# A recurrent attention fused with a squared-ReLU layer: DMA due times in the planner, and the state keys of four chunks by a DMA transpose

## The chip, the cores and the metric

The kernel runs on one core of one Trainium2 chip. The metric is the device time of one execution in microseconds, given as the median of several runs. A core has a matrix engine (PE, with its weight loads shown apart as PEld), a vector engine (DVE), a scalar engine (ACT), GpSimd (POOL), the queue engine SP that issues most DMAs of this kernel, and 16 DMA engines that move the bytes. Each engine takes its instructions in the order of the program; between engines there are semaphores.

## The reference

Four sequences, eight heads, 768 steps, 48 features a head. A gated linear recurrence, then a two-layer MLP on the 3072 tokens with 384 features:

```python
for t in range(S):
    state = alpha[:, :, t, :, None] * state + np.einsum('bhd,bhe->bhde', k[:, :, t], v[:, :, t])
    y[:, :, t] = np.einsum('bhd,bhde->bhe', q[:, :, t], state)
...
x = attn_out.transpose(0, 2, 1, 3).reshape(B * S, H * D)
h = x @ w_in                 # 384 -> 2048
r = np.maximum(h, 0.0)
return (r * r) @ w_out       # 2048 -> 384
```

## The kernel before

**Chunks.** The 3072 tokens are 24 chunks of 128, six to a sequence (chunk s is part c = s mod 6 of its sequence; chunks 5, 11, 17 and 23 are the last of theirs). Inside a chunk the recurrence becomes matrix products. With L the logarithm of alpha and A the exponential of its running sum along the tokens, the scores are (q·A)(k/A)ᵀ under a triangular mask, the state takes (k/A)ᵀv and is then multiplied by A of the last token, and the output is scores·v plus (q·A)·state.

**What a chunk issues, chunk 11 and later (the code calls these raw).** Four loads on SP (`at`, `qt`, `kt`, `vt`, line 371). ACT takes the logarithm of alpha (L396). POOL casts q, k and v to bf16 (L413, L405). Two DMA transposes on SP turn q and k (L416, tile `rawt`). PE forms the running sums twice: `p0` (L435, keys by tokens, one matmul of 384 columns with the triangle as weights, only used for the state) and `pT` (L447, transposed, four matmuls). ACT makes A (L451), 1/A transposed (L454) and, from `p0`, 1/A by tokens (`Ainv`, L466). DVE forms q·A transposed (L507), k/A transposed (L510), and k/A by tokens, `kI` (L505). PE then does the scores (`p2`, tile `sc`), the state update (`ps`, tile `st`, whose weights are `kI`), the product with the previous state (`p3a`, weights from `qkT`, data `sb`) and the masked scores times v (`p3b`). DVE scales the state (L581), ACT copies it to bf16 (L586, `sb`), and ACT copies the output to `xn` (L386). The last chunk of a sequence has no state update, hence no `p0`, `Ainv` and `kI`. Finally `xn` is turned into columns of `xT_big`: by PE and DVE for most chunks, by a DMA transpose on SP (L620) for chunks 18 to 22.

**The MLP.** Tokens go in groups: one of four chunks, two of one, then pairs (8 and 9, and so on to 22 and 23). The first product (weights `w_in_b`, tile `bank<-xT_big,w_in_b`) needs the `xT_big` columns of every chunk of the group. ACT applies ReLU (L676), DVE squares into `gT` (L684), and the second product (`bank<-w_out_b,gT`) is copied out (L758) and stored.

**What sets the order.** A small planner in the kernel sorts every operation before anything is emitted. An operation has an engine, a duration, a latency, the operations it waits for and, where it uses PSUM, a bank. The planner starts on each engine what can start first and gives it a finish time, `op.done = t + op.dur + op.lat`. Loads are a first-in first-out engine "DMA", transposes an engine "TR" whose duration also occupies "DMA"; on the chip both go to SP's one queue. After the planning the operations are sorted by start and emitted, so an engine's order on the chip is the planner's. An operation's `late` is added to its place in the sort alone, not to its finish:

```python
op.start = t + getattr(op, "late", 0.0)
free[eng] = t + op.dur
...
op.done = t + op.dur + op.lat
```

So a longer latency in the planner moves what waits for a DMA further back in the order of its engine; the DMA itself is not slower. A gate holds `p0` (or `pT`, where there is no `p0`) of chunk s back until s is at most LEAD plus the number of MLP tiles done, counting a first and a second product as half a tile each:

```python
return s <= LEAD + (prog["m1"] + prog["m2"]) / 5.12
```

Of the kernel before, what the change touches and what calls it, by code (L numbers as in the profile page):

```python
# [54 lines left out]
def after(op, x=0.0):  # L55
    return (op, x)
# [85 lines left out]
def kernel(  # L142
# [10 lines left out]
    nc = tc.nc  # L153
# [4 lines left out]
    NP = H // 2  # L158
# [35 lines left out]
        out=utri_f, in_=utri_f, compare_op=ALU.is_ge, fill=0.0,  # L194
# [10 lines left out]
    for c in range(JN):  # L205
        blk = slice(JP * c, JP * c + JP)
        nc.gpsimd.affine_select(
            out=tri4[blk, 0:JW], in_=tri4[blk, 0:JW], compare_op=ALU.is_ge, fill=0.0,
# [27 lines left out]
    def pin(ins):  # L236
        tc.keep_in_program_order(ins)
# [12 lines left out]
    GLA_BANKS = sl_bank[0:2]  # L250
# [7 lines left out]
    X_SLACK = 0.2  # L258
    LD = 0.98
    LD1 = 1.0  # L260
    WLD = 2.1
    LAG = 3.2
    SQ_PRIO = 0.0

    def add(eng, dur, emit, *deps, **kw):
        return plan.add(Op(eng, dur, emit, deps, **kw))
# [6 lines left out]
    def load_w(which):  # L273
# [25 lines left out]
        prev = w_cast[-SB] if len(w_cast) >= SB else None  # L299
        ld = add("DMA", WLD * n / 4 + 0.03, e_issue, prev, lat=LAG if which == "o" else 2.0)  # L300
        op = add({"POOL": 0.1 + 0.46 * n, "DVE": 0.1 + 0.2 * n, "ACT": 0.1 + 0.32 * n}, 0, e_cast, ld, prio=-3.0)
# [9 lines left out]
    EARLY = 4  # L311
    RAW = 11
    XTURN = (18, 23)
    TLD, TLAT, TLATE = 1.0, 4.0, 2.0
    NR = 3
    R = {}

    def raw_tiles():
        if R:
            return  # L320
        R["b"] = stage.tile([P, NR, 2, H, DP], BF16, name="rawb", tag="stage")
        nc.gpsimd.memset(R["b"][:, :, :, :, D:], 0.0)
        R["t"] = stage.tile([P, NR, 2, NP, P], BF16, name="rawt", tag="stage")
        R["i"] = stage.tile([P, 2, NP, P], BF16, name="aiT", tag="stage")

# [38 lines left out]
    def add_load(s, nm):  # L364
        d = C[s]
        b, c = divmod(s, NCH)

        def ld():
            if nm not in d:
                d[nm] = loads.tile([P, H, D], FP32, name=nm)  # L370
            pin(nc.sync.dma_start(out=d[nm], in_=SRC[nm][b, c]))
        prev = C[s - LB].get("use_" + nm) if s >= LB else None
        d["ld_" + nm] = add("DMA", LD if s < 4 else LD1, ld, prev, lat=2.0 if s < 4 else LAG if s < 6 else 2.4, at=0.6)

    def add_chunk(s):
        d = C[s]
        b, c = divmod(s, NCH)
        i = s % NBUF
        L, qA, kI, ae = L_s[:, i], qA_s[:, i], kI_s[:, i], ae_s[:, i]
        old = C[s - NBUF].get("end") if s >= NBUF else None  # L380
        g = dict(prio=-10.0 + s * 0.01)
        last = c == NCH - 1

        def cast(op, out_t, in_t):
            if op.eng == "ACT":
                pin(nc.scalar.copy(out_t, in_t))  # L386
            elif op.eng == "DVE":
                pin(nc.vector.tensor_copy(out_t, in_t))  # L388
            else:
                pin(nc.gpsimd.tensor_copy(out_t, in_t))  # L390
# [6 lines left out]
        if joint:  # L397
            ln = J["ln"]
        else:
            ln = [add("ACT", 0.41, e_ln, d["ld_at"], old, prio=-15.0 if s < EARLY else -5.0)]  # L400
# [6 lines left out]
        raw = s >= RAW  # L407
        if raw:
            w, wz = s % NR, s % 2

            def e_rb(j, nm):
                raw_tiles()
                pin(nc.gpsimd.tensor_copy(R["b"][:, w, j, :, 0:D], d[nm]))  # L413

            def e_turn(j):
                pin(nc.sync.dma_start_transpose(out=R["t"][:, w, j], in_=R["b"][:, w, j].rearrange("p h d -> p (h d)")))  # L416
            rt = []
            for j, nm in enumerate(["qt", "kt"]):
                cb = add("POOL", 0.55, lambda j=j, nm=nm: e_rb(j, nm), d["ld_" + nm],
                         *([C[s - NR]["turn"][j]] if s >= RAW + NR else []), prio=-5.0)  # L420
                d["use_" + nm] = cb
                t_ = add("TR", TLD, lambda j=j: e_turn(j), cb, *([C[s - NR]["turned"][j]] if s >= RAW + NR else []), lat=TLAT)
                t_.late = TLATE
# [17 lines left out]
        p0 = Op("PE", 0.66 if joint else 0.17 if raw else 0.27, e_p0, ln, takes=GLA_BANKS, lat=0.05, **g)  # L441
# [14 lines left out]
        def e_aeT(j):  # L456
            rows = slice(64 * j, 64 * j + 64)
            pin(nc.scalar.activation(ae[rows, :, j], d["pmT"][rows, :, P - 1], AF.Exp))
# [11 lines left out]

        def e_ae1():
            pin(nc.scalar.activation(ae[64:128, :, 1], d["pm"][64:128, HD:HD + NP], AF.Exp))
        if not (raw and last):
            plan.add(p0)
        if not raw:
            a_ = add("ACT", 0.38, e_A, p0, **g)
            ai = add("ACT", 0.38, e_Ai, p0, after(a_), **g)
        if raw:
            ai = None
            if not last:  # L480
                ai = add("ACT", 0.38, e_Ai, p0, **g)
                p0.gives = ai
            pT = Op("PE", 0.23, e_pT, [*ln] + ([] if last else [after(p0)]), takes=GLA_BANKS, **g)
            plan.add(pT)
            if last:
                pT.gla = s
            aT = add("ACT", 0.48, e_AT, pT, after(ai) if ai else None, **g)
            aiT = add("ACT", 0.48, e_AiT, pT, after(aT), *([C[s - 2]["turned"][1]] if s >= RAW + 2 else []), **g)
            pT.gives = aiT
            if not last:  # L490
                ae0 = add("ACT", 0.18, lambda: e_aeT(0), pT, after(aiT), **g)
                pT.gives = ae1 = add("ACT", 0.19, lambda: e_aeT(1), pT, after(ae0), **g)
        elif joint:
            ae1 = J["ae"]
            p0.gives = ai
        else:
            ae0 = add("ACT", 0.18, e_ae0, p0, after(ai), **g)
            ae1 = add("ACT", 0.19, e_ae1, p0, after(ae0), **g)
            p0.gives = ae1
# [8 lines left out]

        def e_kiT():
            pin(nc.vector.tensor_mul(d["qkT"][:, NP:2 * NP, :], R["t"][:, w, 1], R["i"][:, wz]))  # L510
        if raw:
            if not last:
                mk = d["use_kt"] = add("DVE", 0.47, e_kI, ai, d["ld_kt"], old, **g)
            cp = add("DVE", 0.34, e_qAT, aT, rt[0], **g)
            cpk = add("DVE", 0.34, e_kiT, aiT, rt[1], cp, **g)
            d["turned"] = [cp, cpk]
        else:
            mq = d["use_qt"] = add("DVE", 0.47, e_qA, a_, d["ld_qt"], old, **g)
            mk = d["use_kt"] = add("DVE", 0.47, e_kI, ai, d["ld_kt"], old, **g)
# [11 lines left out]
        if not raw:  # L531
            p1q = plan.add(Op("PE", 0.22, e_p1q, [mq], takes=GLA_BANKS, **g))
            p1k = plan.add(Op("PE", 0.22, e_p1k, [mk] if s < EARLY else [mk, after(p1q)], lat=0.15,
                              takes=P1K_BANKS if s < EARLY else None, **g))

        def e_cp(lo, hi):
            if "qkT" not in d:
                d["qkT"] = work.tile([P, 2 * NP, P], BF16, name="qkT")
            cast(cpk if lo else cp, d["qkT"][:, lo:hi, :], d["pTk"][:, 0:NP, :] if lo else d["pT"][:, lo:hi, :])
        if s < EARLY:  # L540
            cp = add({"ACT": 0.49, "DVE": 0.34}, 0, lambda: e_cp(0, NP), p1q, **g)
            cpk = add({"DVE": 0.34, "ACT": 0.49}, 0, lambda: e_cp(NP, 2 * NP), p1k, **g)
# [23 lines left out]
        if not last:  # L566
# [7 lines left out]
            prev = C[s - 1].get("sb") if s else None  # L574
            if c == 0 and s:
                prev = C[s - 2]["sb"]
# [41 lines left out]
        if XTURN[0] <= s < XTURN[1]:  # L618
            def e_xt():
                pin(nc.sync.dma_start_transpose(out=xT_big[:, :, s * P:(s + 1) * P], in_=d["xn"]))  # L620
            d["x"] = add("TR", 0.8, e_xt, xn, lat=TLAT)
            d["x"].late = 1.0
            d["end"] = xn
            return
        p4 = plan.add(Op("PE", 0.165, e_p4, [xn], takes=GLA_BANKS, lat=0.14, **g))
# [159 lines left out]
    for d in DMA_ORDER + list(range(6, NT)):  # L785
        if d in ("i", "o"):
            load_w(d)
        elif d == "at":
            add_joint_alpha()
        elif isinstance(d, tuple):  # L790
            add_load(*d)
            if d[0] >= JN:
                if all("ld_" + nm in C[d[0]] for nm, _ in srcs):
                    add_chunk(d[0])
            elif d == JLAST:
                for s in range(JN):
                    add_chunk(s)
        else:
            for nm, _ in srcs:
                if nm != "at":  # L800
                    add_load(d, nm)
                elif d <= 9:
                    add_load(d, nm)
                if nm == "at" and 9 <= d < NT - 1:
                    add_load(d + 1, nm)
            add_chunk(d)
# [24 lines left out]
                b2 = add_last(g, tt, b2, pools) if GT[g] + tt == NT - 1 else add_moe2(g, tt, b2, {}, range(NQ), pools)  # L831
        sq[(g, "free")] = b2

    LEAD = 3.7

    def gate(op):
        s = getattr(op, "gla", None)
        if s is not None:
            return s <= LEAD + (prog["m1"] + prog["m2"]) / 5.12
        return True  # L840
# [18 lines left out]
    for op in plan.order:  # L859
        if op.eng == "PE":  # L860
# [3 lines left out]
            if pe_end is not None and DUMMY and not opened and op.start < CALM:  # L864
                n = max(0, int((op.start - pe_end) / 0.11 + (0.4 if op.start < DENSE else -1.8))) + (extra.pop(0) if extra else 0)
# [35 lines left out]
```

## Time and profile before

| What | Value |
|---|---|
| Median of 3 runs | 186.39 us (184.87 to 186.94) |
| The profiled execution's own time | 185.07 us |
| Its span, first to last instruction | 183.4 us |
| PE busy | 177.5 us (97%), 1908 matmuls |
| DVE, ACT, POOL busy | 127.1, 126.5, 39.4 us |
| SP's hardware queue, share of the 16 DMA engines | 80.7% over the span |
| DMA transposes on SP | 26 of `rawt` (median 3.4 us to landing), 5 of `xT_big` (2.5 us) |

The span leaves out 1.7 us of the device time. The records of matmuls overlap, because each shows its whole way through the array; a 384-column matmul has a record of 326 ns, but the next one starts 0.16 us later. So a busy PE is read by the distances between starts, not by the lengths. Rows of SP are times in which SP issues a DMA, not the time that the data takes; the landing is a separate number.

### The profile page before, as it was taken

What the parts mean: (1) busy time and instruction counts of PE and PEld (TensorE: products, weight loads), DVE (VectorE), ACT (ScalarE), POOL (GpSimd) and SP (SyncE); (2) the same over time, 40 slices, a digit from 0 to 9 for tenths busy, and PEclk for the clock granted to TensorE, in tenths of its full rate; (3) what the DMA queues carried; (4) which work ended last, traced back from release to release, by engine and by line L of the source; (5) the groups of instructions that cost most, each with busy time, mean ns of one, the idle gap of its engine ahead of it and who ended that gap; (6) DMA issues with size and microseconds to landing.
All of it is one profiled execution on the core that took longest, in us unless ns stands there. A gap on an engine that the chain in (4) does not pass through costs nothing.

```text
span 183.4 us, 4946 instructions
## 1 busy us (share of the span) xinstructions
PE 177.5 (97%) x1908; PEld 130.5 (71%) x1908; DVE 127.1 (69%) x273; ACT 126.5 (69%) x286; POOL 39.4 (21%) x80
## 2 busy tenths in 40 slices
PE   7999999899999999999999998999999999999993
PEld 2577884567769877867768776667766777778663
DVE  1179898684999998778877867748855984744200
ACT  3677799226859996966967859847975895767321
POOL 8221100021131142132223133342323512000000
PEclk9999999999999999999999999999999999999999
DMA  5999999999999999998999599898898898901022
GB/s 168 215 212 252 302 366 321 326 220 204 177 191 201 194 179 173 141 190 161 150 193 202 113 240 186 161 227 162 170 201 182 176 163 194 301 13 43 12 77 86
DMA packets 120200, 34.12 MB, mean 186 GB/s; under 512 B 112400, under 2 KB 118928, under 8 KB 120176
## 3 DMA queue, kind: packets, MB, share of 16 engines
q1 hardware_dynamic: 119536, 31.83, 80.7%
q0 software_dynamic: 640, 1.97, 3.2%
q8 instruction: 15, 0.25, 0.6%
q14 instruction: 9, 0.07, 0.2%
HBM read 25.17 MB, written 4.72 MB: 163 GB/s over the span
## 4 chain that ended last, share of the span: by engine, by line
PE 49%; DMA 2%; ACT 1%; issue 0%; DVE 0%
PE bank L240 45%; DMA at<-in_alpha_dram 2%; PE sc L240 2%; PE st L240 1%; PE bank L243 1%; ACT aiT L454 0%; ACT r L676 0%; ACT ob L758 0%; ACT L_s L396 0%; ACT ob L716 0%; DVE xT_big L388 0%; ACT qkT L451 0%
## 5 line engine op out<-in xcount | busy, mean ns | idle before, releaser
L240 PE MATMUL bank<-xT_big,w_in_b 128*128 128x256 bf16 (+2 forms) x636 | 76.6, 262 | 0.9 <-ACT r L676 0.7
L240 PE MATMUL bank<-w_out_b,gT 128*128 128x384 bf16 (+1 forms) x400 | 71.6, 320 | 0.5 <-DVE w_out_b L296 0.5
L676 ACT ACTIVATE r<-bank 128x512 bf16<-128x512 f32 x96 | 56.6, 606 | 11.3 <-PE bank L240 9.9
L240 PEld LDWEIGHTS <-w_in_b 128*128 128x128 bf16 x636 | 52.7, 98 | 10.6 <-issue 1.5
L240 PEld LDWEIGHTS <-gT 128*128 128x128 bf16 x416 | 37.2, 98 | 18.7 <-DVE w_out_b L296 1.0
L684 DVE TENSOR_TENSOR gT<-r 128x512 bf16<-128x512 bf16 x96 | 41.8, 453 | 10.2 <-ACT r L676 9.0
L561 DVE TENSOR_TENSOR sm<-sc,utri_b 128x512 bf16<-128x512 f32 x48 | 30.8, 684 | 5.9 <-PE sc L240 5.7
L405 POOL CAST vb<-vt 128x384 bf16<-128x384 f32 x24 | 13.6, 569 | 69.1 <-DMA vt<-in_v_dram 55.2
L386 ACT CAST xn<-bank 128x384 bf16<-128x384 f32 x24 | 11.6, 482 | 11.6 <-PE bank L240 11.5
L505 DVE TENSOR_TENSOR kI_s<-kt,Ainv 128x384 bf16<-128x384 f32 x21 | 12.8, 611 | 7.8 <-ACT Ainv L466 7.8
L240 PEld LDWEIGHTS <-qkT 64*128 64x128 bf16 (+1 forms) x272 | 10.7, 95 | 6.4 <-issue 2.4
L586 ACT CAST sb<-st 128x384 bf16<-128x384 f32 x20 | 9.6, 482 | 7.7 <-DVE st L581 7.5
L758 ACT COPY ob<-bank 128x384 f32<-128x384 f32 x14 | 6.7, 480 | 8.0 <-PE bank L240 8.0
L396 ACT ACTIVATE L_s<-at 128x384 bf16<-128x384 f32 x20 | 10.5, 527 | 2.4 <-DMA at<-in_alpha_dram 2.3
L240 PE MATMUL bank<-warm 128*128 128x256 bf16 (+1 forms) x54 | 10.9, 348 | 1.3 <-DVE warm L188 1.3
L502 DVE TENSOR_TENSOR qA_s<-qt,A 128x384 bf16<-128x384 f32 x11 | 6.3, 575 | 8.0 <-ACT A L462 8.0
L413 POOL CAST rawb<-qt 128x384 bf16<-128x384 f32 x13 | 7.4, 570 | 20.3 <-DMA qt<-in_q_dram 20.3
L413 POOL CAST rawb<-kt 128x384 bf16<-128x384 f32 x13 | 7.6, 587 | 19.0 <-DMA kt<-in_k_dram 11.1
L581 DVE TENSOR_TENSOR st<-st,ae_s 128x384 f32<-128x384 f32 x20 | 11.1, 556 | 0.5 <-PE st L240 0.5
L466 ACT ACTIVATE Ainv<-bank 128x384 bf16<-128x384 f32 x21 | 10.5, 501 | 1.1 <-PE bank L240 1.0
L240 PE MATMUL sc<-qkT 64*128 64x128 bf16 x192 | 9.5, 219 | 0.0
L240 PEld LDWEIGHTS <-sm 128*128 128x128 bf16 x192 | 8.1, 96 | 1.7 <-issue 0.2
(64 smaller groups left out, 165.7 us busy)
## 6 DMA issues: line engine op xcount, KB each, us to landing
qt<-in_q_dram SPq DMA_DIRECT2D x24, 192.0 KB, 4.0
kt<-in_k_dram SPq DMA_DIRECT2D x24, 192.0 KB, 3.6
vt<-in_v_dram SPq DMA_DIRECT2D x24, 192.0 KB, 3.8
at<-in_alpha_dram SPq DMA_DIRECT2D x20, 192.0 KB, 4.0
wo<-in_moe_w_out_dram SPq DMA_DIRECT2D x4, 768.0 KB, 8.5
out_dram<-ob POOLq DMA_DIRECT2D x10, 192.0 KB, 3.1
wi<-in_moe_w_in_dram SPq DMA_DIRECT2D x4, 384.0 KB, 5.3
wi<-in_moe_w_in_dram SPq DMA_DIRECT2D x2, 768.0 KB, 8.3
```

The costliest lines, as they stand in the source:

```text
L240: pin(nc.tensor.matmul(*a, **kw))
L386: pin(nc.scalar.copy(out_t, in_t))
L396: pin(nc.scalar.activation(L[:, :, 0:D], d["at"], AF.Ln))
L405: pin(nc.gpsimd.tensor_copy(d["vb"], d["vt"]))
L413: pin(nc.gpsimd.tensor_copy(R["b"][:, w, j, :, 0:D], d[nm]))
L466: pin(nc.scalar.activation(d["Ai"], d["pm"][:, 0:HD].rearrange("p (h d) -> p h d", h=H), AF.Exp, scale=-1.0))
L505: pin(nc.vector.tensor_mul(kI[:, :, 0:D], d["kt"], d["Ai"]))
L561: pin(nc.vector.tensor_mul(d["sm"][:, hh], d["sc"][:, hh], utri_b.to_broadcast([P, NP, P])))
L581: pin(nc.vector.tensor_mul(st4, st4, bcast(ae, D)))
L586: pin(nc.scalar.copy(d["sbt"], d["st"]))
L676: pin(nc.scalar.activation(box["r"][:, 0:w], box["ph"][:, 0:w], AF.Relu))
L684: pin(nc.vector.tensor_mul(gT[g][:, f0:f0 + per, lo * P:lo * P + n], r, r))
```

## The change

The planner's numbers first. Loads of chunk 11 and later get a latency of 4.2 instead of 2.4 (alpha 5.2), transposes 6.0 instead of 4.0. The transposes of `xn` take a place in SP's order 2.6 after their due start instead of 1.0. LEAD goes from 3.7 to 4.3.

Then chunks 18 to 21. They no longer have `p0`, `Ainv` and the DVE product `kI` (L505). The gate moves to their `pT`. Instead, once DVE has written k/A transposed into `qkT` (L510), SP issues a DMA transpose of it into the same `kI` buffer, with all 64 columns a head, and `ps` waits for that DMA. In the planner it costs 0.65 and lands 6.0 later.

```diff
+    LT = 4.2
...
-    TLD, TLAT, TLATE = 1.0, 4.0, 2.0
+    TLD, TLAT, TLATE, XLATE = 1.0, 6.0, 2.0, 2.6
+    KTURN = 17
...
-        d["ld_" + nm] = add("DMA", LD if s < 4 else LD1, ld, prev, lat=2.0 if s < 4 else LAG if s < 6 else 2.4, at=0.6)
+        d["ld_" + nm] = add("DMA", LD if s < 4 else LD1, ld, prev, lat=2.0 if s < 4 else LAG if s < 6 else 2.4 if s < RAW else LT + (1.0 if nm == "at" else 0.0), at=0.6)
...
+        kd = KTURN <= s < 22 and not last
+        nat = not (s >= RAW and (last or kd))
...
-        if not (raw and last):
+        if nat:
             plan.add(p0)
...
-            if not last:
+            if nat:
                 ai = add("ACT", 0.38, e_Ai, p0, **g)
-            pT = Op("PE", 0.23, e_pT, [*ln] + ([] if last else [after(p0)]), takes=GLA_BANKS, **g)
+            pT = Op("PE", 0.23, e_pT, [*ln] + ([after(p0)] if nat else []), takes=GLA_BANKS, **g)
             plan.add(pT)
-            if last:
+            if not nat:
                 pT.gla = s
...
+        def e_kn():
+            pin(nc.sync.dma_start_transpose(out=kI.rearrange("p (n a) d -> p n (a d)", a=2),
+                                            in_=d["qkT"][:, NP:2 * NP, :].rearrange("p n t -> p (n t)")))
         if raw:
-            if not last:
+            if nat:
                 mk = d["use_kt"] = add("DVE", 0.47, e_kI, ai, d["ld_kt"], old, **g)
...
+            if kd:
+                mk = add("TR", 0.65, e_kn, cpk, old, lat=TLAT)
+                mk.late = 0.5
...
             d["x"] = add("TR", 0.8, e_xt, xn, lat=TLAT)
-            d["x"].late = 1.0
+            d["x"].late = XLATE
...
-    LEAD = 3.7
+    LEAD = 4.3
```

## The prediction

> **What bounds the kernel now.** I read the page's busy line and slices first, to see which engine is full and where.
>
> ```profile
> span 183.4 us, 4946 instructions
> PE 177.5 (97%) x1908; PEld 130.5 (71%) x1908; DVE 127.1 (69%) x273; ACT 126.5 (69%) x286; POOL 39.4 (21%) x80
> PE   7999999899999999999999998999999999999993
> DMA  5999999999999999998999599898898898901022
> ```
>
> PE is full from the second slice to the last, so time can only be won by work taken off PE or by waits of PE; DMA is nearly as full until slice 35 (about 160 us). The waits of PE alone, from the list of waits, show how little is left:
>
> ```profile
> PE bank L240 <- DVE warm L188: 1.3, 1, 1.3
> PE bank L240 <- ACT r L676: 0.7, 1, 0.7
> PE bank L240 <- DVE w_out_b L296: 0.5, 1, 0.5
> PE bank L243 <- DVE kI_s L505: 0.2, 1, 0.2
> ```
>
> The first and third belong to the start (warm-up, and 32 us), which the change leaves alone. The second is the one place where the chain leaves PE in the stretch that it touches; the chain in order of time, 104 to 112 us, says why:
>
> ```profile
> 105.28 4.13 DMA at<-in_alpha_dram
> 109.40 0.02 issue
> 109.42 0.34 ACT L_s L396
> ...
> 110.70 0.60 ACT aiT L454
> 111.30 0.49 ACT r L676
> 111.79 0.04 issue
> 111.84 0.38 PE bank L240 x2
> ```
>
> Chunk 19's alpha was issued at 105.28, landed at 109.40, and ACT, whose order puts its logarithm there, stood still; the ReLU behind it came late for PE. The second full resource is SP. Its timeline, with start and length of each issue:
>
> ```profile
> 128.73 1.47 SPq L416 DMA_TRANSPOSE rawt<-rawb  x1
> 130.25 0.57 SPq L371 DMA_DIRECT2D kt<-in_k_dram  x1
> 130.92 1.21 SPq L620 DMA_TRANSPOSE xT_big<-xn  x1
> 132.18 0.57 SPq L371 DMA_DIRECT2D vt<-in_v_dram  x1
> 132.80 0.58 SPq L371 DMA_DIRECT2D at<-in_alpha_dram  x1
> 133.49 1.84 SPq L416 DMA_TRANSPOSE rawt<-rawb  x1
> 135.37 0.58 SPq L371 DMA_DIRECT2D qt<-in_q_dram  x1
> 136.06 1.90 SPq L416 DMA_TRANSPOSE rawt<-rawb  x1
> 138.06 1.23 SPq L620 DMA_TRANSPOSE xT_big<-xn  x1
> ```
>
> Each row begins within 0.1 us of the last one's end, and so it goes from 63 to 155 us; the only gaps are 1.36 us at 149 and 0.96 us at 154. An issue of a load takes 0.57 us, of a transpose 1.2 to 3.5 (mean 1.70 over the 26 of `rawt`).
>
> **The change part by part.** *Removed from PE:* `p0` of four chunks. For chunk 18, PE's timeline has it at 121.84 and the next matmul at 122.00, so 0.16 us; 4 × 0.16 = **0.65 us**, all on the path, since PE is full around it. *Removed from ACT and DVE:* four `Ainv` and four `kI`,
>
> ```profile
> L505 DVE TENSOR_TENSOR kI_s<-kt,Ainv 128x384 bf16<-128x384 f32 x21 | 12.8, 611 | 7.8 <-ACT Ainv L466 7.8
> L466 ACT ACTIVATE Ainv<-bank 128x384 bf16<-128x384 f32 x21 | 10.5, 501 | 1.1 <-PE bank L240 1.0
> ```
>
> 4 × 0.50 = 2.0 us of ACT and 4 × 0.61 = 2.4 us of DVE. From 120 to 150 us both are busy for 21 to 22 of 30 us, so I count this at nothing: it is idle time made longer. Without that cover it would be worth up to 2 us.
>
> *Later due times for loads.* Alpha gets 2.8 us more before its logarithm is placed, q, k and v 1.8 more before POOL's casts. Against the 0.71 us that ACT stood idle at 109.4 that is enough, so the wait of 0.66 us at 111.8 should go: **−0.66 us** (bounds 0, if another late landing takes its place, and −0.66). What is late next is the casts and with them the transposes of q and k, which can take it: from the landings of the `rawt` rows and the starts of L510, keys of chunks 18 to 23 landed at 118.5, 124.5, 131.9, 139.6, 146.0, 153.8 and were first used at 124.5, 131.0, 138.4, 144.3, 151.0, 157.2, so 3.4 to 6.5 us early.
>
> *LEAD.* By counting product matmuls in the timeline, `p0` of chunk 19 ran at 128.2 when 16.9 first and 13.75 second tiles were done, a lead of 19 − 15.3 = 3.7; chunks 9 to 22 all show 3.6 to 3.7. The gate binds, and 0.6 tile more, at some 6.6 us a tile (`xn` of 18 to 22 are 6.6 apart), would let a chunk start 4.0 us earlier. But in the planner the turned keys come 1.8 + 2.0 = 3.8 us later, which uses up nearly the same 4 us. So I expect chunks to run 0 to 2 us earlier up to about 20 and up to 2 us later at 22 and 23. That costs no PE time while there is second-product work to put in: when the first product of tiles 18, 20 and 22 began (141.0, 154.3, 163.3), second products were 1.5, 1.5 and 2.5 tiles behind, at 16 × 0.162 = 2.6 us each, a cover of 3.9, 3.9 and 6.5 us. **0.**
>
> *Four key transposes.* Shape and type are those of a `rawt` transpose. DMA engines: the queue moved 31.83 MB in 80.7% of 183.4 us, 215 GB/s, so 128 KB take 0.61 us; four make 2.4 us, where the share from 120 to 150 us is 0.87, which leaves 3.9. SP: each takes 1.2 to 3.5 us of a queue without gaps; with the mean and the 0.08 between rows, 4 × 1.78 = 7.1 us, less the two gaps of 2.3, puts its tail up to 4.8 us later; at the minimum of 1.2, 4 × 1.28 − 2.3 = 2.8. Behind them queue the turned q and k of chunks 20 to 23, the last loads, and the `xn` transposes. The Trainium skill, "Advanced Engine Details and Errata", section "X-Bar Transpose (TRN2)", states that transpose DMAs are as fast as regular ones. By that rule I would estimate 4 × 0.65 = 2.6 us on SP, hidden but for 0.3; the issue rows here do not agree with it (1.70 against 0.57), though the landings do (3.4 us against 3.6 to 4.0).
>
> *The new wait.* `ps` of chunks 18 to 21 now waits for a DMA that begins after L510, and behind it on PE wait the whole MLP and the next chunks. Before, `ps` came about 1 us after L510 (124.5, 125.5). The state is next needed by `p3a` of the following chunk, at 133.4 for chunk 19, so the planner may put `ps` up to 6 us back without harm; it budgets 6.65 us. The nearest rows land 2.3 to 5.9 us after issue (median 3.4), plus the wait in SP's queue, which for `rawt` I read as about 2 us from cast end to issue: typically 5.4, at worst 8. So 0 for three chunks and about one miss of 0.3: **+0.3 us** (bounds 0 and 4 × 1.3 = 5.2).
>
> *The transposes of `xn`.* The `x` of chunk 19 landed at 140.5 and its first product began at 141.0; of 21 at 154.2 and 154.3. These are exactly in time, so lateness here is paid by PE. The change gives 2.0 us more time and places the issue 1.6 us later, so 0.4 net, plus the 0 to 2 us of earlier chunks; against it stands SP's push of 2.8 to 4.8 us by the end. I take **+0.2 us** (bounds 0 and +4.4, the whole push less 0.4), near the low end because the landing rows (2.5 us) are far under the 6.0 now allowed.
>
> **Sum:** −0.65 − 0.66 + 0.3 + 0.2 = −0.8 us. On the profiled execution 185.07 becomes 184.3 (span 182.6). The shown median is 1.32 us above the profiled run; carrying the same difference over, 186.39 − 0.8 = **185.6 us**.
>
> **Rivals.** *Slower: SP's queue decides.* If every key transpose costs SP its mean of 1.78 us and SP can't catch up, two of them lie ahead of chunk 19's `x` or the next (3.6 us) and all four ahead of chunk 21's; PE, in order, stands at the first product of tiles 18 and 20. Less 0.4 of net allowance, that is about 3.2 us at the first and, because PE is then itself later, 1.2 more at the second: 186.39 − 1.3 + 4.4 = 189.5 in full, 188.6 with 0.9 us earlier chunks. It decides from about 3.2 us of waits on. For it: SP has no gaps, and `x` lands in the last moment today. Against: many of SP's long rows contain waits for casts that later due times shorten.
>
> *Faster by more.* The three runs differ by 2.1 us for one program, and the profiled one is near the lowest. If the 1.3 us between it and the median are waits for late landings like the one at 105 us, and the new due times hold them off: 186.39 − 0.65 − 0.66 − 1.3 = 183.8. For it: a load landing between 2.9 and 8.8 us. Against: PE shows almost no such waits, and nothing shown says where the other runs lose.
>
> *It does not bring the lead that it says.* The gate's 4 us and the keys' 3.8 us cancel, another load is late in place of alpha's, and the 0.65 us are spent in waits for keys: 186.4, no change.
>
> **How the numbers follow.** Forecast 0.37, no change 0.10, faster by more 0.25, slower 0.28. A measurement of this kernel can tell about 1% (1.9 us) from nothing. Forecast and no change fall within it (0.47), the other two outside. The range reaches from 183.4, just under the faster case, to 188.9, past the middle of the slower one; the forecast's own range is 184.6 to 186.6.
>
> **What would show it.** Right: no `Ainv` or `p0` at chunks 18 to 21; PE waits near 111 us gone; keys landing within 6 us of L510; `ps` without a wait; SP without gaps and ending near 158 to 160 us rather than 157. Wrong: a PE wait released by a DMA at `st<-vb,kI_s` or at the first product of tiles 18, 20 or 22 totalling over 2 us, key transposes that take SP over 2 us each, or PE waits in new places with the old ones kept.

## The result and the profile after

The change makes the kernel slower. Its median is 187.3 us (185.99 to 188.46, six runs) against 185.2 us for the kernel before in the same set (183.76 to 186.94); the ratio is **1.0137, interval 1.0095 to 1.018**. In this and all comparisons below a ratio leaves out executions more than 1.5% above the fastest of their kernel, so a median can stand further off than its ratio says. The profiled execution took 186.69 us, span 185.0.

The page after, busy line and two rows of the slices:

```profile
span 185.0 us, 4923 instructions
PE 176.0 (95%) x1904; PEld 129.7 (70%) x1904; DVE 124.2 (67%) x270; ACT 124.8 (67%) x281; POOL 38.8 (21%) x80
PE   7799998899999999999999999999998999999993
DMA  5999999999998999979999998798889998941012
```

The work went as foretold: four matmuls fewer, and four `kI` on DVE and four `Ainv` on ACT (the page has three and five records fewer, because one copy of an output moved from ACT to DVE). The span is 1.6 us longer, and PE is busy 1.5 us less. Both numbers have to be split before they are read. Up to the scores of chunk 8 both kernels give PE the same work in the same order, and this execution is already 0.7 us behind there (60.35 instead of 59.69 us); the first 7 us alone have 1.0 us less of busy PE. From that point on the span is 0.9 us longer and PE busy 0.6 us less, which fits the 0.65 of the four `p0`, so PE stands still 1.5 us longer. The ratio stands for some 2.5 us. So this pair of profiles shows where PE waits, but less than half of the loss. The list of PE's waits says for whom:

```profile
PE bank L240 <- DVE warm L188: 1.3, 1, 1.3
PE bank L240 <- DMA xT_big<-xn: 1.1, 2, 0.7
PE bank L240 <- ACT gT L343: 1.0, 1, 1.0
PE bank L240 <- DVE sm L571: 0.7, 2, 0.3
PE bank L240 <- DVE w_in_b L297: 0.6, 1, 0.6
...
PE sc L240 <- DVE qkT L514: 0.2, 1, 0.2
```

The wait for ACT's ReLU of before is gone. The waits of 1.0 and 0.6 us (for `gT` and `w_in_b`) lie at 6 and 29 us, before anything that the change touches; they differ from profile to profile. The new ones of this change are the `xT_big` columns (twice, 1.1 us) and the mask product `sm` (twice, 0.7 us). No wait for a key transpose is there. Where they come from is seen in the chain in order of time, 138 to 168 us, in which PE is not the whole of the path any more:

```profile
139.66 1.22 SPq L420
...
140.93 0.68 SPq L373
...
141.70 1.33 SPq L420
...
143.08 3.49 DMA kt<-in_k_dram
...
146.69 0.56 DVE kI_s L509
147.25 1.21 DVE sm L571 x2
...
148.50 5.06 PE bank L240 x40
...
159.65 6.86 DMA xT_big<-xn
166.51 0.14 issue
166.65 1.36 PE bank L240 x11
```

The chain runs through SP's issues themselves (`SPq`): the k load of chunk 22 could not be issued until 143.08, landed at 146.57, DVE's `kI` for chunk 22 stood in front of the mask product of chunk 21, and PE waited for that. At 159.65 it runs through the `xn` transpose of chunk 22, 6.86 us from issue to landing, and the first product of tiles 22 and 23 begins 0.14 us behind it. SP's own timeline shows the queue in that stretch (start, length):

```profile
133.75 0.57 SPq L373 DMA_DIRECT2D vt<-in_v_dram  x1
134.37 2.56 SPq L373 DMA_DIRECT2D at<-in_alpha_dram  x1
137.03 1.23 SPq L516 DMA_TRANSPOSE kI_s<-qkT  x1
138.36 1.20 SPq L630 DMA_TRANSPOSE xT_big<-xn  x1
139.66 1.22 SPq L420 DMA_TRANSPOSE rawt<-rawb  x1
```

POOL had cast the q of chunk 21 by 134.8, and its transpose (139.66) waited 4.9 us for its turn behind a load, a key transpose (L516) and an `xn` transpose. Before, the same step waited 1.6 us. Nearly half of the 4.9 us is the load of alpha: its row is 2.56 us long where the loads around it have 0.57, and what held it the trace doesn't show.

### The profile page after: what moved, and what is told of

It reads as the page before. It is cut to its first block, busy times and chain, and to the rows that moved or that the text cites. A ratio compares the mean times of both kernels' runs of the same rounds, so it can differ in the third digit from the quotient of the medians.

```text
span 185.0 us, 4923 instructions
## 1 busy us (share of the span) xinstructions
PE 176.0 (95%) x1904; PEld 129.7 (70%) x1904; DVE 124.2 (67%) x270; ACT 124.8 (67%) x281; POOL 38.8 (21%) x80
## 4 chain that ended last, share of the span: by engine, by line
PE 73%; DMA 13%; ACT 4%; DVE 4%; SPq 2%; issue 1%; DVEq 0%; ACTq 0%
PE bank L240 64%; DMA wi<-in_moe_w_in_dram 5%; PE bank L243 4%; PE sc L240 4%; DMA xT_big<-xn 4%; DMA at<-in_alpha_dram 2%; DMA kt<-in_k_dram 2%; PE st L240 2%; SPq L420 1%; DVE sm L571 1%; ACT r L686 1%; DVE kI_s L509 1%; DVE w_in_b L297 1%; DVE w_out_b L297 0%; ACT ob L768 0%
## 5 line engine op out<-in xcount | busy, mean ns | idle before, releaser
L240 PE MATMUL bank<-xT_big,w_in_b 128*128 128x256 bf16 (+2 forms) x636 | 74.8, 262 | 1.8 <-DMA xT_big<-xn 1.1
L694 DVE TENSOR_TENSOR gT<-r 128x512 bf16<-128x512 bf16 x96 | 41.1, 451 | 14.6 <-ACT r L686 14.1
L509 DVE TENSOR_TENSOR kI_s<-kt,Ainv 128x384 bf16<-128x384 f32 x17 | 10.2, 598 | 1.7 <-DMA kt<-in_k_dram 1.4
L240 PE MATMUL bank<-warm 128*128 128x256 bf16 (+1 forms) x54 | 9.6, 316 | 1.3 <-DVE warm L188 1.3
L455 ACT ACTIVATE qkT<-bank 128x512 bf16<-128x512 f32 x13 | 7.9, 605 | 2.9 <-PE bank L240 2.9
L240 PE MATMUL bank<-vb,sm 128*128 128x48 bf16 x192 | 9.1, 183 | 0.7 <-DVE sm L571 0.7
```

The costliest lines, as they stand in the source:

```text
L240: pin(nc.tensor.matmul(*a, **kw))
L455: pin(nc.scalar.activation(d["qkT"][:, NP:2 * NP, :], d["pmT"], AF.Exp))
L509: pin(nc.vector.tensor_mul(kI[:, :, 0:D], d["kt"], d["Ai"]))
L694: pin(nc.vector.tensor_mul(gT[g][:, f0:f0 + per, lo * P:lo * P + n], r, r))
```

## The experiments

Three theories stood at the start. **Queue:** the key transposes take issue time in SP's queue, which is full, and turned keys, loads and `xn` columns come late. **Order:** the new due times and LEAD are what costs. **Wait:** PE stands at the state update for the keys. All ratios are to the kernel before on the same chip.

### The new times without the keys

```diff
-    KTURN = 17
+    KTURN = 99
```

> The change without the four key transposes: chunks 18 to 21 keep p0, Ainv and kI; the longer due times of loads and transposes, the later place of the xn transposes and LEAD 4.3 stay. Queue theory (the loss comes from four more transposes in SP's full queue, which make turned keys and xn columns late): 0 to 1% faster than before, about 184 to 185 us, and the turned q of chunk 21 is issued about 2 us after its cast rather than 5.3. Order theory (the loss comes from the new due times and LEAD themselves, which bring chunks early and use up second-product work that covers late xn columns): 1 to 1.5% slower, like the change, with waits of PE at the first product of tiles 18, 20 or 22. Wait theory (the loss is PE standing at the state update for the keys): same as before.

Measured: 1.0062 (1.0024 to 1.01), median 186.2. So the times alone cost something, 0.6% or 1.1 us, where the queue theory had 0 to 1% faster; the order theory had about twice as much. Less than half of the change's loss. Where it arises isn't known: the only trace of this kernel is of an execution that took 188.84 us, 2.7 above the median.

### The keys alone

```diff
-    LT = 4.2
+    LT = 2.4
...
-    TLD, TLAT, TLATE, XLATE = 1.0, 6.0, 2.0, 2.6
+    TLD, TLAT, TLATE, XLATE = 1.0, 4.0, 2.0, 1.0
...
-                mk = add("TR", 0.65, e_kn, cpk, old, lat=TLAT)
+                mk = add("TR", 0.65, e_kn, cpk, old, lat=6.0)
-    LEAD = 4.3
+    LEAD = 3.7
```

(The extra 1.0 of alpha goes too.)

> The kernel before with the four key transposes alone (their latency in the planner 6.0 as in the change; all other due times, the place of the xn transposes and LEAD as before). Queue theory: slower by 1% or more, 187 us and up, since four issues of 1.3 to 1.8 us go into a queue with 2.3 us of gaps and the tighter due times know less of it. Order theory: 0 to 0.7% faster, by the 0.65 us of p0 that PE no longer does. Wait theory: slower, with PE waits at the state update released by the key transposes.

Measured: 1.0136 (1.0061 to 1.0211), with a median of 189.5 of six runs. As far as the wide interval tells, as slow as the change, as the queue theory has it; the order theory's gain isn't there. In its profile PE waits 1.5 us for the scaled keys (`qkT`, L514) ahead of the scores, 1.5 for the copy of the state and 0.8 for `xT_big`, none directly for a key transpose.

### Four transposes that nobody reads, planned

```diff
...
+            if 17 <= s < 22 and not last:
+                add("TR", 0.65, e_idle, cpk, lat=6.0).late = 0.5   # qkT's key half into a spare tile
```

> The kernel before with four more transposes on SP at the place of the key transposes, from the same tile, into a tile that nobody reads; p0, Ainv and kI stay, nothing waits for the new transposes. Queue theory: slower by 1 to 2% (187 to 189 us), and within 0.65 us plus noise of the kernel with the key transposes alone. Order theory: within 0.5% of before. Wait theory: the same as before, since no instruction waits for them.

Measured: 1.0221 (1.0166 to 1.0277). The wait theory falls as the main cause: nothing waits for these transposes, and they cost no less than the real keys. That the real ones are 0.85% cheaper, since `p0`, `Ainv` and `kI` go, is likely but not shown: the intervals overlap.

### LEAD alone

```diff
-    LEAD = 3.7
+    LEAD = 4.3
```

> The kernel before with LEAD 4.3 in place of 3.7 and nothing else. Queue theory: within 0.7% of before, to either side: no DMA is added, though chunks that start 4 us earlier have less time until their turned keys are due. Order theory: 0.7 to 1.5% slower, second-product work at the start of the first product of tiles 18 and 20 falling from 1.5 tiles to about 1. Wait theory: same as before.

Measured: 1.0037 (0.9997 to 1.0077). Not told apart from nothing, at most 0.8%. The order theory's mechanism did not show: at the first product of tiles 18 and 20 the second products were 2.5 tiles behind, not 1 (before 1.5).

### The same four transposes, with the order of all other engines untouched

Since the planner makes a new order around every added DMA, the last kernels change more than SP. Here the transpose is issued beside the DVE product that makes its input, without telling the planner.

```diff
             pin(nc.vector.tensor_mul(d["qkT"][:, NP:2 * NP, :], R["t"][:, w, 1], R["i"][:, wz]))
+            if 18 <= s < 22:
...
+                pin(nc.sync.dma_start_transpose(out=<spare tile>, in_=<key half of d["qkT"]>))
```

> The kernel before with its order on PE, ACT, DVE and POOL untouched, and in SP's queue, at the place where DVE's k/A transposed of chunks 18 to 21 is due, one more transpose each into a tile that nobody reads. Only SP and the DMA engines have more to do. Queue theory: 1 to 2% slower, PE waits at the first product of tiles 18, 20 and 22 for xn columns, and little different from the same four transposes planned by the planner (ratio 1.022). Planner theory (it is the replanning around more DMA work, not the work, that costs): within 0.5% of before.

Measured: 1.0327 (1.0277 to 1.0377), 191.0 us. The planner theory falls; the work on SP costs by itself, even more than foretold. Half of the 6.1 us is one stall of PE, and it comes by a load. The same row of ACT before, and then three rows of this kernel:

```profile
136.42 0.52 ACT L396 ACTIVATE L_s<-at 128x384 bf16<-128x384 f32 x1 [0.46 <-DMA at<-in_alpha_dram]
...
140.21 0.52 ACT L396 ACTIVATE L_s<-at 128x384 bf16<-128x384 f32 x1 [3.50 <-DMA at<-in_alpha_dram]
...
141.63 0.42 DVE L507 TENSOR_TENSOR qkT<-rawt,qkT 128x512 bf16<-128x512 bf16 x1 [4.33 <-ACT qkT L451]
...
142.79 0.61 PE L240 MATMUL sc<-qkT 64*128 64x128 bf16 x8 [3.13 <-DVE qkT L510]
```

The load is the alpha of chunk 23. SP issued it at 135.40 instead of 132.80, right behind the second added transpose, and it landed at 140.2 instead of 136.4. ACT's order puts its logarithm ahead of the exponentials of chunk 20, so these, DVE's scaling of chunk 20's q and keys, and PE's scores all came late; the turned keys themselves had landed at 133.4. The windows by the microsecond (PE, PEld, DVE, ACT, POOL busy, granted clock, DMA) show what followed on PE:

```profile
142.00:143.00 1.00, 0.21 (x6) 0.21 (x8) 0.64 (x2) 0.77 (x4) 0.44 (x1) 0.61 0.14 27
143.00:144.00 1.00, 1.00 (x14) 0.63 (x11) 0.56 (x1) 0.00 (x0) 0.54 (x1) 0.50 1.08 314
144.00:145.00 1.00, 1.00 (x6) 0.50 (x5) 1.00 (x3) 0.00 (x0) 0.00 (x0) 0.50 1.58 223
145.00:146.00 1.00, 1.00 (x9) 0.70 (x8) 0.20 (x1) 0.48 (x1) 0.13 (x1) 0.68 0.55 120
```

PE stood for 3.13 us until 142.79 and then ran at half its clock until about 145.6. The change itself does not lose its time in this way: its longer due time for alpha leaves that logarithm without a wait. So this run shows that a fuller SP queue costs time, but at a place where the old due times leave none.

### Plain copies in place of the transposes

```diff
-                pin(nc.sync.dma_start_transpose(out=<spare tile>, in_=<key half of d["qkT"]>))
+                pin(nc.sync.dma_start(out=<spare tile>, in_=<key half of d["qkT"]>))
```

> As the last, but plain copies of the same 128 KB inside the chip's memory, from SP at the same places. If SP's issue time decides (0.6 us of a plain issue against 1.3 us of a transpose, so 2.5 instead of 5.2 us in all, against 2.3 us of gaps): 0 to 0.7% slower, half of the transposes' loss or less. If the bytes on the DMA engines decide: as slow as the transposes, 1 to 2%.

Measured: 1.007 (1.0027 to 1.0113). The same bytes at the same places cost a fifth: 0.7% against 3.3%. Its four issues took 0.57 us each on SP in the mean, the transposes 1.21. So it is not the bytes; it is the length of the issue or something else that belongs to transposes. The stall is there too, only shorter: alpha of chunk 23 was issued at 133.58, 0.8 us later than before instead of 2.6, and PE stood 0.97 us for the scores of chunk 20 instead of 3.13.

### The xn transposes back on PE

```diff
-    XTURN = (18, 23)
+    XTURN = (22, 23)
```

> The change with the xn transposes of chunks 18 to 21 back on PE and DVE (three PE transposes and one copy each, as for the other chunks); only chunk 22 keeps its DMA. SP then has four key transposes more and four xn transposes fewer than before. Queue theory: about as before or up to 0.5% faster than it, 184 to 185.5 us, at least 0.8% better than the change, although PE gets 4 x 0.17 us of work back. Order theory: no better than the change without key transposes, 0.6% slower than before, plus 0.7 us for the PE work: 187. Wait theory: as slow as the change.

Measured: 1.0098 (1.0064 to 1.0132). Better than the change by less than hoped (the intervals overlap), and worse than the queue theory said. PE has 4 × 0.17 us more to do than in the change, and the new times' 0.6% are in it, which together would make the 1.0% without anything from SP. Its profile speaks against that: PE waits 1.1 us for scaled keys (`qkT`, L514) and, here alone, 0.9 us for two key transposes at the state update, the wait of the wait theory.

### Six v loads from SP to POOL

```diff
-            pin(nc.sync.dma_start(out=d[nm], in_=SRC[nm][b, c]))
+            pin((nc.gpsimd if nm == "vt" and s >= 18 else nc.sync).dma_start(out=d[nm], in_=SRC[nm][b, c]))
```

> The change with the v loads of chunks 18 to 23 issued by POOL instead of SP, same bytes and same order otherwise (orders on PE, ACT and DVE are those of the change). Queue theory, SP's issue time: six issues of 0.65 us leave SP, 3.9 us of the 5.3 us that the key transposes put in, so most of the loss comes back: within 0.5% of before, unless the issue of 1024 short rows takes POOL so long that its casts come late. Bytes theory: as slow as the change, 1.4%.

Measured: 0.9981 (0.9939 to 1.0022), 184.9 us. This settles it. PE, ACT and DVE have exactly the change's order, the DMA engines the same bytes, the four key transposes are still there; only six issues went to another queue, and 1.6%, or 2.9 us, came back (by the two intervals about 1.8 to 4.0). The time from issue to landing did not get shorter (`xT_big` 3.9 us in the median against 3.5 in the change, the key transposes 4.7 against 3.9); what got shorter is the wait for a turn, for the q of chunk 21 from 4.9 to 2.9 us. A POOL issue of this load took 0.91 us and landed after 4.7 us (median), the SP ones after 3.9, and that was early enough.

### The same on the kernel before, and two more

> The kernel before with the v loads of chunks 18 to 23 issued by POOL instead of SP, nothing else. If SP's queue already costs the kernel before time, it gets faster too, 0.5 to 1%, about 184 us. If SP's queue only costs time once the key transposes are in it, it is within 0.4% of before: PE showed few waits there.

Measured: 1.0009 (0.9972 to 1.0046). So SP's queue, though its rows were back to back, cost the kernel before nothing that can be measured.

> The kernel before with the four key transposes at the old due times and LEAD, and the v loads of chunks 18 to 23 on POOL. Queue theory: its 1.4% loss on SP alone goes to 0.5% or less, perhaps 0.3% faster than before. If the longer due times are what made the change with POOL loads as fast as before (0.998), this one stays at 1% slower or more.

Measured: 0.997 (0.993 to 1.0009): the keys at the old times, with the six loads on POOL. Against the last kernel that is 0.4% faster, 0.7 us; the intervals overlap, but it is the size of the 0.65 us of `p0`. Against the keys alone on SP, 1.7% came back, and with room on SP the new times make no difference that shows.

> The change with the v loads of chunks 11 to 23 on POOL. Queue theory: SP gets another 7 x 0.65 us of room between 63 and 105 us, where nothing was late at PE, so about the same as with chunks 18 to 23 alone, 0.99 to 1.0 of before. If POOL's 0.9 us a load crowds its casts: 0.5% slower than that.

The same line of code with `s >= 11` on the change. Measured: **0.9946 (0.9916 to 0.9975)**, median 184.1: the one version clearly faster than both kernels. Its PE waits are these alone, all at the start:

```profile
PE bank L240 <- DVE warm L188: 1.3, 1, 1.3
PE bank L240 <- DVE w_out_b L297: 0.5, 1, 0.5
PE bank L240 <- DVE w_in_b L297: 0.2, 1, 0.2
```

> The kernel before with the v loads of chunks 11 to 23 on POOL. Queue theory: 0 to 1% faster than before, and not slower than with chunks 18 to 23 alone; the wait for alpha near 109 us goes, since SP issues that load earlier.

On the kernel before: 0.999 (0.9955 to 1.0024). The ReLU's wait near 111 us goes from its profile too, but the time doesn't move measurably. So no gain from room on SP alone can be seen, nor from the end of that wait; together with the change it pays.

## Why the prediction was wrong, point by point

- **The step that failed is the price of SP's push: the +0.2 us for the `xn` columns, and no cost for all else that queues behind the key transposes.** The prediction saw a queue without gaps, worked out a tail 2.8 to 4.8 us later, and then took the low end of its bounds of 0 to 4.4 us. Moving six loads off SP gave 2.9 us back. The reason given for the low price, that `xn` columns land 2.5 us after issue while 6.0 are allowed, counts from the issue; the delay was in front of it, in the queue. The `xn` of chunks 18 to 21 waited 3.8 to 5.6 us for its turn; with six loads on POOL and the same order it waited 1.2 to 3.6.
- **The tail came out at the right size by luck.** The last `xn` transpose began at 159.65 instead of 155.12, 4.5 us later. But its own input was ready only at 158.82 instead of 155.10, so 3.7 us of that is lateness of chunk 22, and 0.8 its turn in the queue. The key transposes' issues took 1.2 to 1.55 us, near the prediction's minimum and not its mean of 1.70.
- **What queued behind was named, but not what it meets.** Turned q and k and loads of chunks 20 to 23 were on the list. The prediction set 3.4 to 6.5 us of earliness against it and entered no cost. That was used up: chunk 21's keys landed at 144.69 and were used at 144.8. And a late k load reached PE by a way that was not on the list, DVE's order: `kI` of chunk 22 in front of `sm` of chunk 21.
- **The cover by second products could not do what the prediction asked of it.** It was counted at 1.5 tiles for tiles 18 and 20 and 2.5 for 22; after the change it is 1.25, 0.75 and 1.75, by counting matmuls as before. But PE takes its matmuls in the planner's order, so the count is fixed before the kernel runs, and no second product can move into a wait that the planner didn't foresee. With v loads on POOL the counts are the same 1.25, 0.75 and 1.75, and the time is not lost. So the entry of 0 for this is not refuted, but its reason is wrong.
- **The slower rival named this mechanism**, with `xn` columns as the place, and 188.6 us, which is 2.2 us above its starting point of 186.39. Measured are 2.5 us by the ratio and 2.1 by the medians, so it was right in kind and close in size (the six runs put the kernel before at 185.2, not 186.39). In part that is luck: it had PE wait 4.4 us at the first products of tiles 18 and 20, and the profile shows 0.7 at tile 18, 0.4 at tile 22 and 0.7 at the mask product. Its chance, 0.28, was too low beside 0.37 for the forecast: the evidence for it (no gaps on SP, columns just in time) was in the text. That the measured time lies in the prediction's wide range is owed to this rival, not to the forecast.
- **Later due times.** The 0.66 us wait did go, as foretold. But the times without the keys are 0.6% slower than before, and the kernel before lost the same wait with v loads on POOL without a gain that shows, so −0.66 was not the term to enter. What the times cost and where stays open; LEAD's share is at most 0.8%.
- **Removed work** is right as far as it can be told: 0.6 us less PE busy in the records from chunk 8's scores on, and 0.7 us, within the noise, between the two kernels with room on SP. With v loads of chunk 11 and later on POOL the change gains 0.5%, 1.0 us, on the kernel before, and 0.4% on the kernel before with the same loads on POOL (the intervals overlap). The sum had 0.8. It may describe the change on a queue that has room; but as its −0.66 is not borne out, the agreement is in part luck.
- **The new wait** at the state update was priced at 0.3 and is not in the list of PE's waits of the change. The transposes landed 2.8 to 5.7 us after issue, and 5.5 to 7.7 us after the product that feeds them, three of the four later than the 6 us that the prediction named as a sign of being right; the planner had put the state update far enough back. With the `xn` transposes on PE there were 0.9 us of this wait.
- **Rule of the skill.** The Trainium skill, "Advanced Engine Details and Errata", section "X-Bar Transpose (TRN2)", has transpose DMAs as fast as regular ones. From issue to landing the runs agree: 3.3 us in the median for the four idle transposes, 3.4 for the four copies. On the issuing queue a transpose took 1.2 us against 0.57 for a plain copy of the same bytes, and the time followed the queue: 3.3% against 0.7%.

That too little room in SP's queue is the cause is shown by the POOL runs: with six issues fewer the loss is gone, and the DMAs behind them are issued sooner, but do not land sooner after their issue. Why the transposes cost nearly five times the copies, with a little over twice the issue, is partly shown: the prediction counted 2.3 us of gaps on SP, which are as long as the copies' 2.3 us of issues and less than half of the transposes' 4.8, and the stalls of 3.13 and 0.97 us follow how late one load of alpha was. Whether transposes also hold up DMAs beside them was not tried alone, nor what made single rows of SP as long as 2.56 us.

## What to carry to other kernels

A queue whose rows stand back to back may still cost nothing, and then the next 5 us in it cost from half their length (2.5 us in the change) to more than all of it (6.1 us with the old due times): look at how long each issue waits behind its input, not only at the time from issue to landing. Work taken from a full engine must be paid for somewhere; here 0.65 us of PE was bought with 5.3 us of the issuing queue. And when PE's order is fixed ahead, work that is planned behind a wait can't fill it. When a DMA is added to a full queue, move another one to an idle queue with it: six loads on POOL made up for the loss, thirteen turned it into a gain of 0.5%.

## What the runs showed of the hardware beyond that

In the run with four unread transposes in an untouched order, the granted clock fell to 0.50 while PE still stood, at about 142.2 by the windows' means, 2.6 us into the stall of 3.13, and stayed there for 0.78 + 1 + 1 + 0.64 = 3.4 us, until about 145.6. For 2.8 us of that PE had work again, which makes 1.4 us of lost clock, nearly half the stall's own length once more. The Trainium skill, "TensorE: Matmul & The Clock Gate", Part 1, tells of an idle window of about 3.4 us after which the array runs at half clock; here the clock fell sooner, so a shorter stall was enough. For the loss of this kernel the clock is not the main thing: the one of its six executions with a mean granted clock of 1.0 took 190.76 us, and one with 0.98 took 190.81.
